# K loads of a later step issued behind both turnings of the key blocks, other slots within a step, and another order of the begin

## The chip, the cores and the metric

The kernel runs on one core of a Trainium2 chip. The metric is the device time of one execution in microseconds (us). TensorE (PE) multiplies matrices, VectorE (DVE), ScalarE (ACT) and GpSimd (POOL) work on tiles, and SyncE (SP) issues nearly all the DMAs of this kernel, one behind the other.

## The reference

Three layers in a chain, over B=4 batches, H=8 heads, S=768 positions and D=48 columns, which are 3072 tokens of 384 columns for the two layers behind.

```
k_n = k / (np.linalg.norm(k, axis=-1, keepdims=True) + 1e-06)
for t in range(S):
    y[:, :, t] = np.einsum('bhd,bhde->bhe', q[:, :, t], state)
    v_old = np.einsum('bhde,bhd->bhe', state, kt)
    state = state + bt[:, :, :, None] * np.einsum('bhd,bhe->bhde', kt, vt - v_old)
...
p = domain_probs / (domain_probs.sum(-1, keepdims=True) + 1e-09)
for e in range(E):
    h = np.maximum(x @ w1[e], 0.0)
    out += p[:, e:e + 1] * (h @ w2[e])
...
expert_idx = np.argmax(logits, axis=1)
for e in range(E):
    mask = expert_idx == e
    h = np.maximum(x[mask] @ w1[e], 0.0)
    out[mask] = gate_w[mask, None] * (h @ w2[e])
```

The first layer is attention by the delta rule. The second is a mixture of 4 experts, all of which see every token. The third has 8 experts, and each token goes to the one that its logits choose.

## The kernel before, in words

The attention is cut into 12 steps of 64 positions. Within a step the recurrence is solved for all positions at once: the Gram matrix of the keys (`gram_k`, L312) gives a triangular system, which DVE inverts in small pivots (`inverse`, L417 and L421), and products with the inverse give z, y and w (`solve_z`, `solve_y`, `solve_w`, L457). What leaves a step are its outputs (`outputs`, L576 and L579, then `columns`, which casts them into the tile xT, L163 and L164) and the new state (`state`, `keep_state`, L561 to L565). Numbers are kept as pairs of f16 halves, hi and lo, so that nearly every product is three matmuls.

The dense layer has 16 pieces per step (4 experts by 4 parts), and each piece is a first product (`first`, L900, with the ReLU on ACT, L904, and its low half on DVE, L905) and a second one (`second`, L922, with the sum into acc on DVE, L932). The dense pieces of one step are what PE does while the next step's attention is prepared. A step has 32 slots, two around each dense piece:

```
for i in range(16 * NS):
    ...
    if i % 16 < 15:
        hidden(i + 1)
    for g in at[2 * i]:
        g()
    dense.second(i, H.pop(i))
    for g in at[2 * i + 1]:
        g()
```

Every engine runs what it is given in the order of this loop; nothing is scheduled later. Which piece of the attention, of the routing or of the weights stands at which slot is written in tables at the head of the file: SLOTS for a step, SECOND for step 1, ROUTE for the routing of the sparse layer, WSLOTS for the third layer's weights, DENSE and KINDS for the splitting of the 32 weight tiles of the dense layer in the first interval (KINDS names the engines: in A, ACT makes the high half and a scaled copy and POOL the low half; in B, ACT makes the high half and DVE the low one; in C, ACT makes the high half, POOL the scaled copy and POOL the low half). WAYS names the engine that spreads results into block form ("S" a DMA of SP, "A" a copy on ACT, "V" a copy on DVE). ORDER is the order of the steps of the begin, before the first dense piece. A negative slot counts back from the start of its own step's interval.

The pieces that bear on the step boundary are these. `load_k` loads the keys of the following step into Kr (L176, 8 DMAs on SP). `split_k` cuts keys into halves KB (ACT L236, then DVE or POOL L238), for two halves x of the heads. `turn_k` turns KB[x] into KTB[x] by one transposing DMA of SP (L288). `sum_k` adds the halves of KTB on DVE into KQ (L305), and `gram_k` multiplies on PE (L312). `expand(0)` (e0) and `expand(1)` (e1) spread the solved columns Ws into WB (L525 on SP, L527 on ACT, L532 on DVE), which `outputs` reads. In the begin, `split_t` makes the halves TB of the inverse (ACT L446, DVE L450), and phi and plo make those of the masked products PT (ACT L385, POOL L388). Of the third layer's weights, wst is loaded (L1090), split on ACT (L1096, L1097) and POOL (L1098), and stored to DRAM as wimg (L1103).

Of the kernel before, what the change touches and what calls it, by code (L numbers as in the profile page):

```python
# [17 lines left out]

SLOTS = dict(load_k=-6, load_q=16, load_v=36, norm=(2, 2, 3, 4), split_k=(-24, -7), turn_k=(-14, -5),
             sum_k=(-5, -1), gram_k=(-2, 0), to_lanes=0, scale=0, split_g=(1, 4), split_q=(-4, -4), turn_q=0,
             gram_q=(5, 6), split_p=(8, 7), expand_s=(8, 10, 12, 14), init=5, pivots=(4, 6, 3, 3, 5, 5, 2, 3, 0),
             from_lanes=13, split_t=15, rest=(15, 17), z=19, save=19, y=21, e0=22, w=24, e1=24, state=25, keep=25,
             out=28)

SECOND = dict(load_k=0, load_q=18, load_v=34, norm=(14, 17, 17, 18), split_k=(-14, -7), turn_k=(-11,
              -7), sum_k=(-5, -1), gram_k=(-2, 0), to_lanes=0, scale=1, split_g=(7, 11), split_q=(-4, -4), turn_q=-3,
              gram_q=(9, 10), split_p=(12, 13), expand_s=(4, 3, 7, 8), init=1, pivots=(4, 0, 4, 0, 4, 1, 4, 4, 1, 2,
              5, 2), from_lanes=13, split_t=15, rest=(10, 16), z=17, save=17, y=19, e0=25, w=21, e1=22, state=24,  # L30
              keep=26, out=30)

ROUTE = dict(first=(0, 4, 7, 9, 9, 10, 10), rest=(2, 6, 11, 16, 20, 24, 27))
WAYS = dict(e0="S", e1="A", sb="SSAA", apply="V", klow="PV")
WSLOTS = dict(back=0, six=(7, 10, 13, 18, 20, 27), seven=(4, 7, 11, 13, 18, 20, 27))


HEAD = dict(loads=(2, 4, 7, 14, 21))
KINDS = "AAADABABABBBABBAABAABACCABCABBBB"
DENSE = dict(w=(0, 0, 1, 1, 1, 2, 3, 3, 3, 5, 6, 7, 7, 9, 10, 11, 13, 15, 15, 15, 16, 17, 20, 21, 22, 23,  # L40
             25, 25, 26), r=13, t=23, e=22, c=26, i=21, p=5, load=0, keep=1)


ORDER = """
cq cw ck0 zk1 load0 twin zk0 ck1 v0 za load1 zt zs0 zk2 load2 zw units square root scale square1 heads wide0 wide1
khi0 klo0 khi1 klo1 tk00 tk01 sum00 sum01 tk10 tk11 sum10 sum11 gd0 gd1 lanes lscale go0 go1 qhi0 qhi1 qscale zs1
tree tf0 root1 W00 W01 P P P P P P P P P P n1 n2 side qrest0 qrest1 n3 n4 n5 heads1 P P P P P wide10 wide11 tf1
khi10 klo10 khi11 klo11 gq0 q1 gq1 ag0 ag1 tk100 load3 tk101 tk110 tk111 mask0 phi0 mask1 P P P P P P P P P P P P
plo0 phi1 plo1 P P P P lanesback thi0 thi1 thi2 thi3 tlo0 tlo1 tlo2 sidelo tlo3 q1hi0 q1hi1 q1lo0 q1lo1 tq1 gate z
W02 save sum100 y e00 ylo v1 load4 e01 e02 e03 W20 W21 W22 sum101 w e10 gk0 sum111 gk0o e11 e12 e13 out0 W10 W11 W12  # L50
out1 columns sum110
"""


class Attention:
# [166 lines left out]
    def norm_apply(self):  # L222
        K = self.K
        eng = self.nc.gpsimd if WAYS["apply"] == "P" else self.nc.vector
        eng.tensor_tensor(out=K, in0=K, in1=self.r0.unsqueeze(2).to_broadcast([128, 16, 48]), op=ALU.mult)
# [4 lines left out]
    def split_k(self, s, x):  # L230
        nc, KB = self.nc, self.keys(s)[x]
        for q in range(4):
# [3 lines left out]
            nc.scalar.activation(out=hi, in_=src, func=AF.Copy)  # L236
            low = self.nc.gpsimd if WAYS["klow"][x] == "P" else self.nc.vector
            low.tensor_tensor(out=KB[r, 1, :, 64 * h:64 * h + 48], in0=src, in1=hi, op=ALU.subtract)  # L238
# [279 lines left out]
    def expand(self, f):  # L518

        for q in range(4):  # L520
            dst, src = self.part_w(f, q)
            how = WAYS["e1" if f else "e0"]
            if how == "S":
# [68 lines left out]
    def pieces(self, s):  # L592
# [5 lines left out]
        def at(slot, *fs):  # L598
            for f in fs:
                p.append((slot, f))  # L600
# [11 lines left out]
        each = lambda f: [lambda x=x: f(x) for x in two]  # L612
        P = SLOTS if s > 1 else SECOND
        if s > 1:
            N = SECOND if s == 2 else SLOTS
            for x in two:
# [15 lines left out]
        for n in range(4):  # L632
            f = self.expand_s if s > 1 and WAYS["sb"][n] == "A" else self.expand_d
            at(P["expand_s"][n], lambda n=n, f=f: f(*divmod(n, 2)))
# [763 lines left out]
def kernel(ctx, tc, q, k, v, beta, probs, w1, w2, emb, tau, v1, v2, out, NA=6):  # L1398
# [16 lines left out]
    def loads(lo, hi):  # L1415
        for n in range(lo, hi):
            dense.load_w(n, nc.sync)

    def head_loads(i):
        loads((0, *HEAD["loads"])[i], HEAD["loads"][i])  # L1420
        if i == 4:
            dense.load_p()
# [12 lines left out]
    at[0].append(attn.state_first)  # L1435
    at[DENSE["keep"]].append(attn.keep_first)
    for s in range(1, NS):
# [3 lines left out]
    for s in range(NS - 1):  # L1441
        for o, g in zip(ROUTE["rest"] if s < NS - 2 else ROUTE["first"], sparse.route_pieces(s, dense)):
            at[32 * (s + 1) + o].append(g)
    at[DENSE["load"]].append(lambda: loads(HEAD["loads"][-1], 32))
    for n, o in enumerate(DENSE["w"]):
        at[o].insert(n + 1 if o == 0 else len(at[o]), lambda n=n + 32 - len(DENSE["w"]): dense.split_w(n, KINDS[n]))
    at[DENSE["r"]].append(lambda: sparse.setup_d(sp, dense.ap))
    at[DENSE["r"] + 1].append(lambda: sparse.setup_r(sp, dense.ap))
    at[DENSE["t"]].append(sparse.setup_t)
# [10 lines left out]
    def w_load(n):  # L1460
        raw[n] = sparse.w_load(sp, *chunks[n])

    def w_split(n):
        cut[n] = sparse.w_split(sp, *chunks[n], raw.pop(n))

    def w_store(n):
        sparse.w_store(*chunks[n], cut.pop(n))
        if n + 2 < len(chunks):
            w_load(n + 2)

    at[29].append(lambda: (w_load(0), w_load(1)))
    six, seven = WSLOTS["six"], WSLOTS["seven"]
    slots = [32 * s + o for s in range(1, NS - 1) for o in (six if 2 <= s < 7 else seven)]
    for n in range(len(chunks)):
        at[slots[n]].append(lambda n=n: w_split(n))
        at[slots[n] + WSLOTS["back"]].append(lambda n=n: w_store(n))

# [127 lines left out]
```

## Time and profile before

| | |
|---|---|
| three runs | 1204.96, 1207.42, 1208.01 us, median 1207.42 |
| profiled execution | 1208.4 us, of which the span of its trace is 1206.7 |
| PE busy | 1125.0 us, 93% of the span |
| weight loads (PEld) | 877.8 us, 73% |
| DVE busy | 807.1 us, 67% |
| ACT busy | 656.7 us, 54% |
| POOL busy | 422.2 us, 35% |
| DMA from and to HBM | 148 GB/s over the span |

The span is the time from the first to the last instruction of the trace; the profiled execution's own time holds 1.7 us around it. Busy times are shares of the whole span. In the page's 40 slices PE is busy in nine tenths or more of each slice but the first ones, and its granted clock is full but for three of the first four (8, 5 and 8 tenths), where the begin and the first dense pieces lie.

### The profile page before, as it was taken

How to read it: one execution, taken by the hardware profiler on the slowest of the kernel's cores; microseconds unless marked ns; L12 is line 12 of the kernel's file. 1: busy time of each engine (PE TensorE's matmuls, PEld its weight loads, DVE VectorE, ACT ScalarE, POOL GpSimd, SP SyncE). 2: the span in 40 equal slices, each digit the busy share in tenths (PEclk: the TensorE clock that was granted, in tenths of full speed). 3: DMA queues.
4: the chain of work that ended last, by engine and by line, in shares of the span. 5: the costliest groups of instructions: out<-in, count | busy, mean ns of one | idle time of the engine just before them, and what ended most of it. 6: DMA issues, size and time to landing. Idle time of an engine off the chain costs nothing. (4 is left out here: it accounts for less than half of the span.)

```text
span 1206.7 us, 33186 instructions
## 1 busy us (share of the span) xinstructions
PE 1125.0 (93%) x12906; PEld 877.8 (73%) x12906; DVE 807.1 (67%) x2859; ACT 656.7 (54%) x1268; POOL 422.2 (35%) x394
## 2 busy tenths in 40 slices
PE   2488999999998999999999999999999999999997
PEld 2466677777777777777777777777777777788775
DVE  8778788687786877868779788797773543222121
ACT  6667675666666665666666675666553142222221
POOL 5647533251332523425135251342411213222221
PEclk8598999999999999999999999999999999999999
DMA  9983345644666346545565475565721195969951
GB/s 218 218 205 75 71 97 149 108 100 118 108 149 113 90 123 109 123 89 119 144 101 148 96 147 142 103 154 105 133 73 28 37 346 133 345 174 283 310 131 29
DMA packets 294672, 167.24 MB, mean 139 GB/s; under 512 B 241396, under 2 KB 276040, under 8 KB 294512
## 3 DMA queue, kind: packets, MB, share of 16 engines
q1 hardware_dynamic: 288656, 154.91, 55.6%
q0 software_dynamic: 4768, 9.98, 2.7%
q8 instruction: 103, 1.69, 0.6%
q14 instruction: 57, 0.47, 0.1%
q10 hardware_dynamic: 1088, 0.20, 0.1%
HBM read 142.54 MB, written 35.90 MB: 148 GB/s over the span
## 5 line engine op out<-in xcount | busy, mean ns | idle before, releaser
L900 PE MATMUL ph<-xT,W 128*128 128x256 f16 x2808 | 334.4, 274 | 4.0 <-POOL W L885 2.4
L922 PEld LDWEIGHTS <-H 128*128 128x128 f16 x2304 | 221.4, 98 | 138.1 <-issue 6.5
L922 PE MATMUL po<-W,H 128*128 128x384 f16 x1728 | 308.7, 328 | 5.1 <-DVE H L905 3.0
L900 PEld LDWEIGHTS <-W 128*128 128x128 f16 x2808 | 271.1, 98 | 45.5 <-POOL W L885 2.9
L904 ACT ACTIVATE H<-ph 128x512 f16<-128x512 f32 x192 | 113.2, 590 | 155.8 <-PE ph L900 151.0
L905 DVE SCALAR_TENSOR_TENSOR H<-ph,H 128x512 f16<-128x512 f32 x192 | 131.1, 686 | 78.0 <-ACT H L904 74.8
L1098 POOL TENSOR_TENSOR wso<-wst,wso 128x768 f16<-128x768 f32 x64 | 105.2, 1644 | 199.7 <-ACT wst L1097 192.3
L1373 DVE SCALAR_TENSOR_TENSOR H<-ph,H 128x512 f16<-128x512 f32 x54 | 37.4, 692 | 156.3 <-ACT H L1372 156.3
L1368 PE MATMUL ph<-xt,slot 128*128 128x128 f16 x1944 | 114.7, 221 | 4.0 <-DMA xt<-g 4.0
L1368 PEld LDWEIGHTS <-slot 128*128 128x128 f16 x1944 | 112.3, 99 | 7.9 <-issue 4.7
L421 DVE TENSOR_TENSOR tt<-tt,pr 128x60 f32<-128x60 f32 (+34 forms) x660 | 111.3, 209 | 0.7
L417 DVE TENSOR_TENSOR pr<-tt,KQ 128x60 f32<-128x60 f32 (+34 forms) x660 | 109.7, 203 | 0.8
L1385 PE MATMUL po<-slot,H 128*128 128x384 f16 x648 | 109.9, 326 | 0.0
L378 POOL TENSOR_TENSOR AO<-O,AO 32x256 f16<-32x256 f32 x48 | 47.0, 980 | 161.7 <-ACT AO L377 159.7
L922 PE MATMUL po<-Wlate,H 128*128 128x384 f16 x576 | 101.2, 326 | 0.7 <-DVE acc L932 0.7
L1096 ACT ACTIVATE wso<-wst 128x768 f16<-128x768 f32 x64 | 53.7, 840 | 71.0 <-DMA wimg<-wso 42.9
L1385 PEld LDWEIGHTS <-H 128*128 128x128 f16 x648 | 62.1, 98 | 38.3
L1390 POOL DMA_INDIRECT out_dram<-ob,idx x27 | 27.3, 1010 | 164.6 <-ACT ob L1389 125.7
L900 PE MATMUL ph<-xT,Wlate 128*128 128x256 f16 x648 | 78.2, 276 | 2.2 <-POOL Wlate L885 2.2
L1372 ACT ACTIVATE H<-ph 128x512 f16<-128x512 f32 x54 | 32.2, 597 | 80.9 <-PE ph L1368 80.9
L900 PEld LDWEIGHTS <-Wlate 128*128 128x128 f16 x648 | 63.3, 99 | 13.1 <-POOL Wlate L885 2.4
L1389 ACT ACTIVATE ob<-po,sm 128x384 f32<-128x384 f32 x27 | 15.7, 580 | 81.4 <-PE po L1385 81.3
(309 smaller groups left out, 1615.6 us busy)
## 6 DMA issues: line engine op xcount, KB each, us to landing
slot<-wimg SPq DMA_DIRECT2D x108, 768.0 KB
wst<-in_moe_w_dram SPq DMA_DIRECT2D x65, 384.0 KB
wimg<-wso SPq DMA_DIRECT2D x64, 384.0 KB
xb<-xr SPq DMA_DIRECT2D x48, 98.0 KB
Qr<-in_q_dram SPq DMA_DIRECT2D x24, 192.0 KB
Vr<-in_v_dram SPq DMA_DIRECT2D x96, 48.0 KB
W<-in_moe_w_dram SPq DMA_DIRECT2D x11, 384.0 KB
Kr<-in_k_dram SPq DMA_DIRECT2D x84, 48.0 KB
```

The costliest lines, as they stand in the source:

```text
L378: self.low.tensor_tensor(out=lo, in0=src, in1=hi, op=ALU.subtract)
L417: nc.vector.tensor_tensor(out=p, in0=t[:, :, j:j + 1].to_broadcast([128, m, j]), in1=AT[:, j, 0:j].unsqueeze(1).to_broadcast([128, m, j]), ...
L421: nc.vector.tensor_tensor(out=t, in0=t, in1=p, op=ALU.subtract)
L900: nc.tensor.matmul(ph[:, i], w1[:, a, k, 128 * i:128 * i + 128], xT[:, b, k], start=(n == 0), stop=(n == 8))
L904: nc.scalar.activation(out=H[:, 0], in_=ph, func=AF.Relu)
L905: nc.vector.scalar_tensor_tensor(out=H[:, 1], in0=ph, scalar=0.0, in1=H[:, 0], op0=ALU.max, op1=ALU.subtract)
L922: nc.tensor.matmul(po[t], H[:, a, i, 128 * t:128 * t + 128], w2[:, b, i], start=(f == 0 and i == 0 and n == 0), stop=(f == 3 and i == 1 an ...
L1096: self.nc.scalar.activation(out=o[:, 0], in_=t, func=AF.Copy, scale=scale)
L1098: self.nc.gpsimd.tensor_tensor(out=o[:, 1], in0=t, in1=o[:, 0], op=ALU.subtract)
L1368: nc.tensor.matmul(ph[:, i], w[:, a, k, 128 * (i % 2):128 * (i % 2) + 128], xt[:, 3 * b + k], start=(m == 0), stop=(m == 8))
L1373: nc.vector.scalar_tensor_tensor(out=H[:, 1], in0=ph, scalar=0.0, in1=H[:, 0], op0=ALU.max, op1=ALU.subtract)
L1385: nc.tensor.matmul(po, H[:, a, i], w[:, b, i % 2], start=(q == 0 and i == 0 and m == 0), stop=(q == 1 and i == 3 and m == 2))
```

## The change

Only the tables change; no instruction is written differently, and the sizes of all tiles stay. In a step, `load_k` goes from slot -6 to -3, behind the turning of the second half x (which stays at -5), the turning of the first half from -14 to -12, `split_k` from (-24, -7) to (-23, -6), `sum_k` of the first half from -5 to -7, the outputs from slot 28 to 29, and e0 from 22 to 24; other pieces move by a slot or a few. The spreading e0 goes from SP's DMAs to DVE copies, e1 from ACT copies to SP's DMAs. The weight tiles 11, 22 and 26 of the dense layer change kind, and many of them their slot (tile 26 from slot 21 to 20). In the begin, several steps trade places. The first lines of the tables, and those of the short ones:

```diff
-SLOTS = dict(load_k=-6, load_q=16, load_v=36, norm=(2, 2, 3, 4), split_k=(-24, -7), turn_k=(-14, -5),
+SLOTS = dict(load_k=-3, load_q=17, load_v=34, norm=(2, 2, 3, 4), split_k=(-23, -6), turn_k=(-12, -5),
...
-WAYS = dict(e0="S", e1="A", sb="SSAA", apply="V", klow="PV")
-WSLOTS = dict(back=0, six=(7, 10, 13, 18, 20, 27), seven=(4, 7, 11, 13, 18, 20, 27))
+WAYS = dict(e0="V", e1="S", sb="ASSA", apply="V", klow="PV")
+WSLOTS = dict(back=1, six=(7, 10, 12, 19, 22, 25), seven=(0, 6, 10, 13, 15, 24, 27))
...
-HEAD = dict(loads=(2, 4, 7, 14, 21))
-KINDS = "AAADABABABBBABBAABAABACCABCABBBB"
+HEAD = dict(loads=(2, 5, 5, 14, 19))
+KINDS = "AAADABABABBAABBAABAABAACABAABBBB"
```

SP at a step boundary before, from the spreading of w to the loads of V (Kr the keys of the next step but one, KB and KTB the halves and the turned keys of the coming step, xb rows of the dense layer's output that go out, wst and wimg the third layer's weights):

```order
L525 DMA WB<-Ws 32x8x48 x8
L176 DMA Kr<-in_k_dram 32x8x48 x8
L288 DMA_TRANSPOSE KTB_165<-KB_150 128x16x128
L1185 DMA xb<-xr_5220 64x392 x2
L1185 DMA xb<-xr_5221 64x392 x2
L1103 DMA wimg<-wso 128x1536
L1090 DMA wst<-in_moe_w_dram 128x3x256
L274 DMA_TRANSPOSE KQ<-QT 128x8x64 x4
L185 DMA Vr<-in_v_dram 32x8x48 x8
```

And the same place in the changed kernel:

```order
L525 DMA WB<-Ws 32x8x48 x8
L1103 DMA wimg<-wso 128x1536
L1090 DMA wst<-in_moe_w_dram 128x3x256
L288 DMA_TRANSPOSE KTB_165<-KB_150 128x16x128
L1185 DMA xb<-xr_5275 64x392 x2
L1185 DMA xb<-xr_5276 64x392 x2
L176 DMA Kr<-in_k_dram 32x8x48 x8
L274 DMA_TRANSPOSE KQ<-QT 128x8x64 x4
L185 DMA Vr<-in_v_dram 32x8x48 x8
```

The eight loads of K have moved from ahead of the transposition of KB to behind it and behind the four DMAs of xb. The eight DMAs of WB at the top are e0 before and e1 after.

ACT over the same stretch before, from the split of w (Ws) to the dense piece behind the split of K:

```order
L512 ACTIVATE Ws<-psw 64x384 x2
L527 ACTIVATE WB<-Ws 32x2x8x48 x4
L564 ACTIVATE SC_171<-S_169 128x384
L564 ACTIVATE SC_172<-S_170 128x384
L236 ACTIVATE KB_152<-Kr 32x8x48 x4
L904 ACTIVATE H<-ph 128x512
```

And in the changed kernel:

```order
L512 ACTIVATE Ws<-psw 64x384 x2
L904 ACTIVATE H<-ph 128x512
L1096 ACTIVATE wso<-wst 128x768
L1097 ACTIVATE wst<-wst 128x768
L564 ACTIVATE SC_171<-S_169 128x384
L564 ACTIVATE SC_172<-S_170 128x384
L904 ACTIVATE H<-ph 128x512
L236 ACTIVATE KB_152<-Kr 32x8x48 x4
```

The four copies into WB have left ACT, and a pair of weight splits and two ReLUs now stand ahead of the split of K.

ACT in the begin before, from the masked products to the first cast of z:

```order
L385 ACTIVATE PT_167<-Wlate 128x512
L385 ACTIVATE PT_168<-Wlate 128x512
L446 ACTIVATE TB<-H 32x16x16x2 x4
L259 ACTIVATE QT<-Qr 128x8x48 x2
L163 ACTIVATE Ws<-psz 128x384
```

And in the changed kernel:

```order
L385 ACTIVATE PT_167<-Wlate 128x512
L446 ACTIVATE TB<-H 32x16x16x2 x4
L259 ACTIVATE QT<-Qr 128x8x48 x2
L385 ACTIVATE PT_168<-Wlate 128x512
L163 ACTIVATE Ws<-psz 128x384
```

The second high half of PT has moved behind the four copies of TB and the two of QT; on POOL its low half (L388) follows it.

## Rows read from the trace of the kernel before

**Rows 1.** TensorE's waits by releaser: total us, times, longest.

```profile
PE ps L312 <- DVE KQ L305: 11.9, 8, 3.0
```

**Rows 2.** Timeline of TensorE: start, us, instruction, count, [idle before, releaser].

```profile
52.95 1.38 PE L312 MATMUL ps<-KQ,KTB 128*128 128x64 f16 x23 [0.42 <-DVE KQ L305]
...
236.49 1.72 PE L312 MATMUL ps<-KQ,KTB 128*128 128x64 f16 x24 [2.21 <-DVE KQ L305]
238.02 3.19 PE L922 MATMUL po<-W,H 128*128 128x384 f16 x12
...
389.65 1.39 PE L312 MATMUL ps<-KQ,KTB 128*128 128x64 f16 x24 [3.02 <-DVE KQ L305]
390.85 3.57 PE L922 MATMUL po<-W,H 128*128 128x384 f16 x12
...
466.93 1.17 PE L312 MATMUL ps<-KQ,KTB 128*128 128x64 f16 x24 [1.59 <-DVE KQ L305]
467.93 2.12 PE L922 MATMUL po<-W,H 128*128 128x384 f16 x12
```

**Rows 3.** A window's busy times: PE, PEld, DVE, ACT, POOL; clock, DMA.

```profile
390.40:393.80 3.40, 3.40 (x25) 1.88 (x22) 2.56 (x4) 2.19 (x7) 0.71 (x2) 0.50 1.16 185
```

**Rows 4.** Timeline of SP's queue at the boundary near 385 us.

```profile
364.28 5.70 SPq L525 DMA_DIRECT2D WB<-Ws  x8
375.20 3.79 SPq L176 DMA_DIRECT2D Kr<-in_k_dram  x8
379.09 4.24 SPq L288 DMA_TRANSPOSE KTB<-KB  x1
```

**Rows 5.** Timeline of VectorE at the same boundary.

```profile
372.26 2.90 DVE L238 TENSOR_TENSOR KB<-Kr,KB 32x384 f16<-32x384 f32 x4 [2.26 <-ACT KB L236]
...
382.57 1.14 DVE L932 SCALAR_TENSOR_TENSOR acc<-po,p,acc 128x384 f32<-128x384 f32 x2
389.17 0.76 DVE L305 TENSOR_TENSOR KQ<-KTB 128x512 f16<-128x512 f16 x2 [5.46 <-DMA KTB<-KB]
```

**Rows 6.** Timelines of SP and TensorE at the boundary before step 2.

```profile
144.84 1.71 SPq L288 DMA_TRANSPOSE KTB<-KB  x1
146.60 5.95 SPq L176 DMA_DIRECT2D Kr<-in_k_dram  x8
...
154.96 4.09 PE L900 MATMUL ph<-xT,W 128*128 128x256 f16 x36
158.88 0.86 PE L312 MATMUL ps<-KQ,KTB 128*128 128x64 f16 x24
```

**Rows 7.** Timeline of ScalarE ahead of the boundary at 464 us.

```profile
446.18 3.40 ACT L527 ACTIVATE WB<-Ws 32x768 f16<-32x768 f16 x4 [0.61 <-DVE Ws L515]
```

**Rows 8.** Timelines of POOL, ScalarE, VectorE and TensorE in the begin.

```profile
40.69 2.27 POOL L388 TENSOR_TENSOR PT<-Wlate,PT 128x512 f16<-128x512 f32 x2
40.77 0.63 ACT L385 ACTIVATE PT<-Wlate 128x512 f16<-128x512 f32 x1 [0.60 <-POOL Wlate L339]
41.31 2.60 ACT L446 ACTIVATE TB<-H 32x512 f16<-32x512 f32 x4
41.97 2.96 DVE L450 TENSOR_TENSOR TB<-H,TB 32x512 f16<-32x512 f32 x3 [1.43 <-ACT TB L446]
45.55 0.69 DVE L450 TENSOR_TENSOR TB<-H,TB 32x512 f16<-32x512 f32 x1
46.30 1.06 PE L457 MATMUL psz<-R,TB 128*128 128x48 f16 x22 [0.52 <-DVE TB L450]
```

**Rows 9.** Timelines of POOL and TensorE in the first interval.

```profile
114.32 0.20 PE L457 MATMUL psz<-R,TB 128*128 128x48 f16 x1 [4.94 <-ACT R L478]
116.02 4.01 PE L900 MATMUL ph<-xT,W 128*128 128x256 f16 x18
...
129.90 2.13 POOL L883 TENSOR_SCALAR Wlate<-Wlate 128x768 f32<-128x768 f32 x1 [2.04 <-issue]
134.17 3.40 PE L900 MATMUL ph<-xT,Wlate 128*128 128x256 f16 x16 [2.17 <-POOL Wlate L885]
```

More of the change, by code (lines that the diff above doesn't have):

```diff
@@ L17 @@
 DRAM = bass.MemoryType.DRAM
-SLOTS = dict(load_k=-6, load_q=16, load_v=36, norm=(2, 2, 3, 4), split_k=(-24, -7), turn_k=(-14, -5),
[L22 to L31, printed above, removed]
@@ L33 @@
-ROUTE = dict(first=(0, 4, 7, 9, 9, 10, 10), rest=(2, 6, 11, 16, 20, 24, 27))
-WAYS = dict(e0="S", e1="A", sb="SSAA", apply="V", klow="PV")
-WSLOTS = dict(back=0, six=(7, 10, 13, 18, 20, 27), seven=(4, 7, 11, 13, 18, 20, 27))
-HEAD = dict(loads=(2, 4, 7, 14, 21))
-KINDS = "AAADABABABBBABBAABAABACCABCABBBB"
-DENSE = dict(w=(0, 0, 1, 1, 1, 2, 3, 3, 3, 5, 6, 7, 7, 9, 10, 11, 13, 15, 15, 15, 16, 17, 20, 21, 22, 23,
-             25, 25, 26), r=13, t=23, e=22, c=26, i=21, p=5, load=0, keep=1)
-ORDER = """
@@ L45 @@
[L45 to L49, printed above, removed]
@@ L50 @@
-W02 save sum100 y e00 ylo v1 load4 e01 e02 e03 W20 W21 W22 sum101 w e10 gk0 sum111 gk0o e11 e12 e13 out0 W10 W11 W12
-out1 columns sum110
+SLOTS = dict(load_k=-3, load_q=17, load_v=34, norm=(2, 2, 3, 4), split_k=(-23, -6), turn_k=(-12, -5),
+             sum_k=(-7, -1), gram_k=(-2, 0), to_lanes=0, scale=3, split_g=(0, 3), split_q=(-6, -2), turn_q=-2,
+             gram_q=(5, 6), split_p=(9, 7), expand_s=(9, 10, 13, 15), init=5, pivots=(3, 6, 4, 4, 4, 4, 1, 5),
+             from_lanes=13, split_t=15, rest=(15, 18), z=20, save=21, y=21, e0=24, w=23, e1=24, state=25, keep=25,
+             out=29)
@@ new lines @@
+SECOND = dict(load_k=0, load_q=21, load_v=31, norm=(14, 17, 17, 18), split_k=(-14, -7), turn_k=(-11,
+              -3), sum_k=(-5, -1), gram_k=(-2, 0), to_lanes=1, scale=1, split_g=(7, 11), split_q=(-4, -4), turn_q=-3,
+              gram_q=(9, 10), split_p=(12, 13), expand_s=(6, 5, 9, 10), init=1, pivots=(3, 0, 4, 1, 6, 0, 5, 4, 0, 3,
+              5), from_lanes=12, split_t=15, rest=(9, 16), z=17, save=17, y=19, e0=26, w=21, e1=22, state=24, keep=26,
+              out=30)
+ROUTE = dict(first=(3, 3, 6, 9, 9, 11, 11), rest=(4, 6, 12, 16, 20, 23, 28))
@@ new lines @@
+WAYS = dict(e0="V", e1="S", sb="ASSA", apply="V", klow="PV")
+WSLOTS = dict(back=1, six=(7, 10, 12, 19, 22, 25), seven=(0, 6, 10, 13, 15, 24, 27))
+HEAD = dict(loads=(2, 5, 5, 14, 19))
+KINDS = "AAADABABABBAABBAABAABAACABAABBBB"
+DENSE = dict(w=(0, 0, 1, 1, 3, 3, 4, 4, 5, 5, 6, 7, 7, 9, 10, 11, 13, 15, 15, 16, 16, 17, 20, 20, 22, 24,
+             25, 25, 25), r=13, t=28, e=22, c=24, i=21, p=5, load=0, keep=1)
+ORDER = """
+ck0 load0 cw zk1 twin zk0 ck1 v0 cq load1 zt units square za root scale square1 heads wide0 wide1 khi0 klo0 khi1
@@ new lines @@
+klo1 tk00 tk01 sum00 sum01 zs0 load2 tk10 tk11 sum10 sum11 gd0 zk2 gd1 lanes lscale P zw go1 qhi0 qhi1 qscale zs1
+tree tf0 root1 W00 P W01 P P P P P P P n1 n2 side qrest0 P go0 qrest1 n3 n4 n5 heads1 P P P wide10 P wide11 tf1
+khi10 q1 P klo10 khi11 klo11 gq0 gq1 ag0 ag1 tk100 load3 tk101 tk110 P P P P P tk111 P P mask0 phi0 mask1 P P P P P
+P P plo0 P P lanesback thi0 thi1 thi3 thi2 tlo0 tlo1 sidelo tlo3 tlo2 q1hi0 q1hi1 q1lo0 q1lo1 tq1 phi1 plo1 gate z
+save W02 sum100 y e00 ylo W20 W21 v1 load4 e02 e01 e03 sum101 w e10 gk0 gk0o e11 e12 e13 out0 W10 W11 out1 W22
@@ L52 @@
+columns sum111 sum110 W12
 """
```

## The prediction, made before the result was known

> **What bounds the kernel now.** I read the busy shares first: TensorE is busy 93% of the span, so what can be won is what it waits. Then I read its waits by releaser. Beside those of the begin, the largest entry that returns is the Gram matrix of the keys, L312, waiting for the sum of the turned halves on VectorE, L305: eight waits, 11.9 us [rows 1]. One, of 0.42, is in the begin; the other seven, 11.5 us together, stand at step boundaries, and the timeline of TensorE shows three of them, 2.21, 3.02 and 1.59 [rows 2].
>
> A wait here costs more than its length. Undisturbed, the 24 matmuls of a Gram matrix take 0.86 [rows 6]; behind a wait they take 1.17, since the second half's sum comes while the first is multiplied, and after the waits of 2.21 and 3.02 they take 1.72 and 1.39, and the dense piece behind takes 3.19 and 3.57 where the third shows 2.12 [rows 2]. In the window behind the wait of 3.02 the granted clock is 0.50 [rows 3], which is 1.2 instead of 2.4 GHz. So the price of the seven is 11.5 + 5 x 0.31 (five waits without a clock loss) + 1.93 + 1.98 (two with one: 0.86 + 1.07, and 0.53 + 1.45) = **17.0 us**.
>
> Why VectorE is late, one boundary tells. It has nothing to do between the end of acc, 382.57 + 1.14 = 383.71, and the sum at 389.17, for which the DMA into KTB releases it [rows 5]. That transposition stands on SP behind the eight loads of K, which start at 375.20, when VectorE's split of KB has just ended (372.26 + 2.90 = 375.16), and take 3.79 to issue; the transposition is issued from 379.09 [rows 4, 5]. From there to the sum are 10.1 us, though its issue takes 4.24.
>
> **What the change does at a boundary.** The eight loads go behind the transposition: it can be issued when KB is ready. KB itself changes its time: its split stands one slot later, and a slot is (466.93 - 389.65) / 32 = 2.4 us [rows 2]; ScalarE loses the four copies into WB, 3.40 [rows 7], and gets about 2.3 ahead of the split (two passes over a weight tile and a ReLU). So KB is ready between 1.1 earlier and 2.4 later; I take 0.8 later, since the split's input waits for no slot but its engine's queue. The issue then comes 379.09 - 375.20 - 0.8 = 3.1 earlier. The second part is the data: the loads' packets no longer lie ahead of the transposition's. The issue of the loads bounds it by 0 to 3.8; I take 2, half. Together the sum comes 5 us earlier, more than the longest wait, 3.02. Nothing waits for the loads of K at their new place: they are split 12 slots, 29 us, on (from slot -3 to slot -23 of the step after).
>
> The Trainium skill, page "DMA: Bandwidth & Descriptors", section "Queues, rings and completion order", says that on each DMA engine descriptors are consumed in ring order. By it all of the loads' data stands ahead of the transposition's, and the order of issue is the order of the data; by the issue times alone only 3.1 would be won. The trace's 10.1 us from issue to sum, against an issue of 4.24, agrees with the ring order but does not prove it.
>
> What is late next is VectorE's own chain. The outputs go from slot 28 to 29, behind a dense piece that was in front of them, so 2.12 us of PE's work between outputs and Gram matrix are gone. The chain's end was at 383.71, and PE was free for the Gram matrix at 389.65 - 3.02 = 386.63: 2.9 of slack, less 2.1 is 0.8, less about 0.4 for the first half's sum is 0.4. The boundary before step 2 is a control for both: there the outputs already stand directly in front, the transposition is issued at 144.84 with the loads of K behind it at 146.60, and neither the 36 matmuls of the dense piece at 154.96 nor the Gram matrix at 158.88 wait [rows 6]. But there the low half of Q's split lay ahead of the outputs, and now it lies in the chain. I reserve **+2.0** for all boundaries (0 if the slack holds, +4.5 if each of eleven is 0.4 late).
>
> The engines of the spreadings, costed: e1 leaves ScalarE and becomes eight DMAs, 5.70 to issue [rows 4]; the outputs stand five slots, 12 us, behind, so 5.7 and some 2 to land leave about 4 us. e0 takes four copies on VectorE, which is busy 67%, five slots ahead of the outputs as well. I cost both at nothing; without that cover each costs its own length, once a step. The other slots (sums, pivots, weights, routing) I cost at nothing too: between boundaries TensorE has work queued, and its waits there are short.
>
> **The begin.** z starts its main part at 46.30, released by TB on VectorE [rows 8]. ScalarE's TB copies begin at 41.31, right behind the second high half of PT (40.77, 0.63), which had waited 0.60 for POOL. In the new order that pass comes later: 0.63 earlier at least. VectorE's three subtractions into TB take 2.96, though a single one takes 0.69: 0.9 too much, while POOL is in L388 from 40.69 to 42.96. With the second L388 moved behind, that falls away. Together **-1.5**; bounds -0.4 (the ScalarE part half hidden, VectorE as before) and -2.0.
>
> The Trainium skill, page "SBUF — State Buffer", section "SBUF: two separate sides", calls the port pair of VectorE and GpSimd an exclusive lock: the loser blocks for the whole instruction. The 2.96 that end right behind 42.96 plus two single lengths agree with it. By it the 0.9 is won in full, without it perhaps nothing, and the begin gives 0.6. It speaks against e0 as copies on VectorE too, where GpSimd works beside them.
>
> **The first interval.** TensorE waits 2.17 at 134.17 for the low half of a weight tile, and its 16 matmuls then take 3.40 [rows 9]; 36 undisturbed ones take 4.09 [rows 6], so 16 take 1.8 and 1.6 is lost to the clock. The tile is number 26, of kind C, with 2.13 on POOL for the scaled copy. It becomes kind A and stands a slot earlier: either would do. That is -3.8; a reserve of 1.0 for tiles 27 and 28, which move, gives **-2.7** (0 to -3.8). The wait of 4.94 at 114.32, behind which 18 matmuls take 4.01 [rows 9], ends with ScalarE's cast of R; its chain loses one low half on VectorE (tile 11) and one pass on ScalarE (tile 22), about 1 us each. I take **-1.1** (0 to -3).
>
> **Sum.** -17.0 + 2.0 - 1.5 - 2.7 - 1.1 = -20.3. From the profiled execution's 1208.4 (span 1206.7 and 1.7 around it) that gives 1188.1. The median of the runs shown, 1207.42, is 1.0 below the profiled one, so **1187**.
>
> **Rivals.** *Half of it.* Only the order of issue is won, and the split of KB is the full slot late: 3.9 - 2.4 = 1.5 earlier. Of the waits 3.02, 2.21 and 1.59, 1.5, 0.7 and 0.1 remain, for seven about 3, with the half sums' 0.31 seven times and one clock loss of 2: 7 us stay. 1194; if begin and first interval give nothing either, 1199. For it speaks the slot; against, the copies that leave ScalarE.
>
> *The chain on VectorE takes the wait over.* If outputs, Q's low half, acc and sum end 1.5 us too late at each of eleven boundaries, 16.5 us come back, and with the clock the time is 1204 to 1209: no change. It decides from 1.9 us of lengthening (0.4 slack). Against it stands the control [rows 6].
>
> *Slower: the outputs wait for e1's DMAs.* If the eight issues stand on SP behind a transposition and weight loads and land 7 us later than I take, TensorE waits 3 at each of ten steps, with a clock loss of 2 each (as for 3.02): 50 us less 20, but half of the steps would do: 1212. It decides when the landing is some 5.5 us late (1.5 waited and 1 to 2 of clock, ten times, is 25 to 35). Against it: SP is free from 369.98 to 375.20 behind e0's own DMAs, which leave [rows 4].
>
> **How the numbers follow.** This kernel's measurement can tell about 0.3%, 3.6 us, from no change. Forecast as summed 0.60, with its own range 1182 to 1193; half of it 0.24; the chain 0.08; slower 0.08. The range holds forecast and half-case: 1181 to 1201. Faster (below 1203.8) 0.85, within 0.3% 0.07, slower 0.08.
>
> **What would show it.** In the profile after: L312 waiting for L305 at no boundary but by tenths; the transposition issued within 1 us of the split's end and landing within 6; the loads of K behind xb; no window at half clock at a boundary; z's main part near 44.8; no wait for POOL near 134. I am wrong if the waits stay under another name: L900 waiting for xT, L576 or L579 for WB, or psz for R.

## The result, and the profile after

The changed kernel takes 1176.51 us (median of four runs, 1174.98 to 1178.80), the kernel before 1206.19 beside it: ratio 0.9755, 95% interval 0.9729 to 0.9780. It is faster by 29.7 us where 20.3 were forecast, and below the range. The profiled executions say the same: spans of 1177.0 and 1206.7. TensorE is busy for 1114.6 us instead of 1125.0, so 10.4 of the gain is busy time and 19.3 is idle time.

Read from the two timelines (the starts of the dense pieces, L900), the gain lies here, in us:

| stretch | change | forecast |
|---|---|---|
| begin, to the first dense piece (60.74, now 59.79) | -0.95 | -1.5 |
| first interval, to its end (154.96, now 149.72) | -4.29 | -3.8 |
| ten boundaries, each from the first dense piece of an interval to the fifth | -14.81 | -15.0 |
| the last four pieces of these ten intervals (nine of them gain) | -3.59 | 0 |
| the pieces between | -3.87 | 0 |
| last interval and last stage | -2.17 | 0 |

These are two single executions. Traces of kernels with the same tables differ by up to 0.8 in the begin and by 2 to 3 in the pieces between and in the last stage; the last four pieces repeat to 0.1 in the traces with the changed tables that have none of the pauses told of below.

The waits of TensorE by releaser in the changed kernel, with what answers to [rows 1] and the other large ones (columns as there):

```profile
PE psz L457 <- ACT R L478: 3.8, 1, 3.8
...
PE ps L312 <- DMA KQ<-QT: 2.3, 2, 1.4
...
PE ps L312 <- DVE KQ L305: 0.9, 2, 0.5
```

The 11.9 of [rows 1] are 0.9, of which one wait of 0.52 stands at a boundary. In exchange two waits of L312 for Q's transposition, 1.43 and 0.92, are new. The boundary of [rows 4, 5], now at 366 to 379 us, in the timelines of SP and then of TensorE:

```profile
365.95 2.92 SPq L288 DMA_TRANSPOSE KTB<-KB  x1
368.97 5.18 SPq L1185 DMA_DIRECT2D xb<-xr  x4
374.21 4.84 SPq L176 DMA_DIRECT2D Kr<-in_k_dram  x8
379.16 5.53 SPq L274 DMA_TRANSPOSE KQ<-QT  x4
```

```profile
372.31 4.09 PE L900 MATMUL ph<-xT,W 128*128 128x256 f16 x36
376.24 0.86 PE L312 MATMUL ps<-KQ,KTB 128*128 128x64 f16 x24
376.94 2.12 PE L922 MATMUL po<-W,H 128*128 128x384 f16 x12
```

The transposition is issued ahead of the loads, the Gram matrix follows the 36 matmuls without a wait and takes 0.86 instead of 1.39, and the piece behind takes 2.12 instead of 3.57 [rows 2]: at this boundary, in these two executions, 5.15 us.

The begin and the first interval, from the timelines that answer to [rows 8, 9]:

```profile
40.62 1.15 POOL L388 TENSOR_TENSOR PT<-Wlate,PT 128x512 f16<-128x512 f32 x1
40.49 2.62 ACT L446 ACTIVATE TB<-H 32x512 f16<-32x512 f32 x4 [0.39 <-DVE H L432]
41.17 1.86 DVE L450 TENSOR_TENSOR TB<-H,TB 32x512 f16<-32x512 f32 x2 [0.71 <-ACT TB L446]
43.65 1.41 DVE L450 TENSOR_TENSOR TB<-H,TB 32x512 f16<-32x512 f32 x2
45.12 1.06 PE L457 MATMUL psz<-R,TB 128*128 128x48 f16 x22 [1.24 <-DVE TB L450]
```

```profile
129.04 2.13 PE L900 MATMUL ph<-xT,Wlate 128*128 128x256 f16 x18
```

z starts its main part at 45.12 instead of 46.30, 1.2 earlier; the first two subtractions, one of them beside POOL's first pass, still take 1.86, against 1.41 for the two that run alone. The tile that TensorE had waited 2.17 for is there, and the 18 matmuls run at full clock.

### The profile page after: what moved, and what is told of

It is laid out like the page before. It is cut to its first block, busy times and chain, and to the rows that moved or that the text cites. A ratio compares the mean times of both kernels' runs of the same rounds, so it can differ in the third digit from the quotient of the medians.

```text
span 1177.0 us, 33182 instructions
## 1 busy us (share of the span) xinstructions
PE 1114.6 (95%) x12906; PEld 873.3 (74%) x12906; DVE 805.4 (68%) x2902; ACT 619.6 (53%) x1227; POOL 409.1 (35%) x393
## 5 line engine op out<-in xcount | busy, mean ns | idle before, releaser
L900 PE MATMUL ph<-xT,W 128*128 128x256 f16 x2808 | 334.0, 274 | 3.9 <-POOL W L885 2.4
L922 PEld LDWEIGHTS <-H 128*128 128x128 f16 x2304 | 219.4, 98 | 134.6 <-DVE H L905 5.1
L922 PE MATMUL po<-W,H 128*128 128x384 f16 x1728 | 306.5, 327 | 3.9 <-DVE H L905 1.7
L900 PEld LDWEIGHTS <-W 128*128 128x128 f16 x2808 | 273.3, 98 | 49.0 <-POOL W L885 2.7
L922 PE MATMUL po<-Wlate,H 128*128 128x384 f16 x576 | 101.3, 326 | 0.3 <-DVE acc L932 0.3
L378 POOL TENSOR_TENSOR AO<-O,AO 32x256 f16<-32x256 f32 x48 | 35.8, 745 | 125.6 <-ACT AO L377 122.9
L900 PE MATMUL ph<-xT,Wlate 128*128 128x256 f16 x648 | 76.7, 272 | 0.5 <-DVE Wlate L886 0.5
L900 PEld LDWEIGHTS <-Wlate 128*128 128x128 f16 x648 | 61.8, 98 | 9.5 <-DVE Wlate L886 0.7
```

Of the source, the lines that this page charges most:

```text
L378: self.low.tensor_tensor(out=lo, in0=src, in1=hi, op=ALU.subtract)
L900: nc.tensor.matmul(ph[:, i], w1[:, a, k, 128 * i:128 * i + 128], xT[:, b, k], start=(n == 0), stop=(n == 8))
L922: nc.tensor.matmul(po[t], H[:, a, i, 128 * t:128 * t + 128], w2[:, b, i], start=(f == 0 and i == 0 and n == 0), stop=(f == 3 and i == 1 an ...
```

## The experiments

Each group of runs stands on one chip, beside runs of the kernel before on it; a ratio is to those. Chips differ: the medians of the kernel before are 1204 to 1214 us on them.

**One number of the change.**

```diff
-SLOTS = dict(load_k=-6, load_q=16, load_v=36, norm=(2, 2, 3, 4), split_k=(-24, -7), turn_k=(-14, -5),
+SLOTS = dict(load_k=-3, load_q=16, load_v=36, norm=(2, 2, 3, 4), split_k=(-24, -7), turn_k=(-14, -5),
```

> The kernel before with one number changed: load_k from slot -6 to -3. Theory L (the loads' place on SP is what made TensorE wait at the boundaries): the seven waits of L312 for L305, 11.5 us, vanish with their half-sums and clock losses, some 13 to 17 us, 1189 to 1193 us, ratio 0.986 to 0.989. Theory E (the boundary was won by everything else that makes KB or the chain on VectorE earlier): within 0.3% of before, since KB, the outputs and the copies on ScalarE stay. Beside either: the loads now end later, and the squares of K (L199) in slot 2 read them; if that is the new wait of the changed kernel, ScalarE waits for Kr at one or two boundaries by 2 to 4 us and some 1 to 3 us come back.

Measured: 1195.51, ratio 0.9852 (0.9828 to 0.9876). Theory L: no wait of L312 for L305 is left at a boundary, and the ten stretches at the boundaries shrink by 17.4 in all (5.15 at the one shown above, as in the changed kernel). VectorE's split of KB and SP at that boundary:

```profile
367.69 2.90 DVE L238 TENSOR_TENSOR KB<-Kr,KB 32x384 f16<-32x384 f32 x4 [2.26 <-ACT KB L236]
```

```profile
370.66 1.73 SPq L288 DMA_TRANSPOSE KTB<-KB  x1
379.88 4.42 SPq L176 DMA_DIRECT2D Kr<-in_k_dram  x8
```

The transposition is issued 0.06 behind the end of the split, at this boundary and at eight others; in the kernel before it was 3.9 to 5.6 behind it at eight boundaries. The squares of K wait for Kr three times here, 1.9 together, so little comes back. One number gives some 18 of the 29.7 us.

**The same number taken out of the changed kernel.**

```diff
-SLOTS = dict(load_k=-3, load_q=17, load_v=34, norm=(2, 2, 3, 4), split_k=(-23, -6), turn_k=(-12, -5),
+SLOTS = dict(load_k=-6, load_q=17, load_v=34, norm=(2, 2, 3, 4), split_k=(-23, -6), turn_k=(-12, -5),
```

> The changed kernel with load_k back at slot -6, all else as changed. Theory L: the waits of L312 for L305 come back, and 10 to 17 us with them, 1187 to 1193 us. Theory E: the split of KB and the chain on VectorE are early enough by themselves: 1176 to 1180. Under both the squares of K no longer wait for Kr, which gives back 1 to 2 us.

Measured: 1230.27, ratio 1.0153 (1.0120 to 1.0186): slower than before, and far outside both theories' numbers. Its TensorE at a boundary, and the window behind the wait (columns as [rows 3]):

```profile
391.78 1.72 PE L312 MATMUL ps<-KQ,KTB 128*128 128x64 f16 x24 [3.62 <-DVE KQ L305]
393.31 4.03 PE L922 MATMUL po<-W,H 128*128 128x384 f16 x12
```

```profile
391.50:400.00 8.50, 8.09 (x58) 5.41 (x58) 3.00 (x5) 2.50 (x8) 1.32 (x2) 0.62 0.63 108
```

L312 waits nine times for L305, 23.6 together; two of these are in the begin. Of the seven at boundaries, six, of 2.8 to 4.4 us, have a clock of 0.50 behind them for about 3 to 6 us (0.62 is the mean of the longer window above), and four boundaries lose 6.5 to 7.4 each against the changed kernel. Some 15 us of the distance to it are not the loads' but that chip's (the pauses shown with the changed kernel's second run). SP at the boundary shown:

```profile
376.19 3.81 SPq L176 DMA_DIRECT2D Kr<-in_k_dram  x8
380.10 0.39 SPq L1103 DMA_DIRECT2D wimg<-wso  x1
380.53 0.43 SPq L1090 DMA_DIRECT2D wst<-in_moe_w_dram  x1
381.07 6.86 SPq L288 DMA_TRANSPOSE KTB<-KB  x1
```

In the changed tables a store of wimg and a load of wst stand ahead of the transposition too. So it is issued 4.9 behind the split of KB instead of 3.9 as in the kernel before, and its issue takes 6.86 instead of 4.24 [rows 4]: the loads in front cost more than before. What makes that issue longer isn't shown. The other edits do not replace the move; they rest on it.

**w a slot earlier, alone.**

```diff
-             from_lanes=13, split_t=15, rest=(15, 17), z=19, save=19, y=21, e0=22, w=24, e1=24, state=25, keep=25,
+             from_lanes=13, split_t=15, rest=(15, 17), z=19, save=19, y=21, e0=22, w=23, e1=24, state=25, keep=25,
```

> The kernel before with w alone moved from slot 24 to 23, so that a dense piece more stands between the product w and the state that reads its halves Ws. Theory W (the 48 matmuls into pss take 1.67 us instead of 1.37 because they start on the halves of Ws just as VectorE finishes them): 0.30 us less in each of nine steps, 2.7 us or 0.22%, and pss at 1.37 in the trace. Rival: pss is slow for the spreading copies on ScalarE that read Ws at the same time; then pss stays at 1.67 and the time within 0.1%.

Measured: 1211.17, ratio 0.9995 (0.9970 to 1.0020). The 48 matmuls into pss did become fast (13.7 us for all 480, from 15.3), as theory W says; ScalarE's copies still run beside them, so the rival is out. Nothing was won all the same: psw now waits for Y, 8.2 instead of 1.0.

```profile
PE psw L457 <- DVE Y L481: 8.2, 11, 1.6
```

In the same execution L312 waits 5.1 for L305 instead of 11.9. Whether w gives that, or the execution, one trace can't tell: these waits differ between executions (see the next run).

**The begin and the dense weights alone**: the tables HEAD, KINDS, DENSE and ORDER of the changed kernel in the kernel before.

> The kernel before with the tables HEAD, KINDS, DENSE and ORDER of the changed one, that is the begin and the splitting of the dense weights alone. If these make what the changed kernel gains up to the end of the first interval: the first dense piece 0.9 earlier, the end of the first interval 5.2 earlier, 1201 us, ratio 0.9955; the boundaries stay as before. If a part of the 4.3 in the first interval came from the moves of the attention's pieces there (table SECOND), 1203 to 1205.

Measured: 1207.81, ratio 0.9957 (0.9930 to 0.9983). By its trace the first dense piece comes 1.50 earlier and the end of the first interval 2.56 earlier, not 5.2: the first interval itself gains 1.06, not 4.29. The wait of 2.17 for the weight tile is gone, but TensorE waits there for another tile, the halves eh that the routing needs, and the matmuls behind take 4.00 instead of 2.15:

```profile
132.06 0.23 PE L1049 MATMUL ps<-ident,eh 8*128 8x8 f16 x3 [1.02 <-ACT eh L937]
133.78 0.24 PE L1049 MATMUL ps<-ident,eh 8*128 8x8 f16 x3 [1.50 <-DVE eh L938]
134.31 4.00 PE L922 MATMUL po<-Wlate,H 128*128 128x384 f16 x12 [0.28 <-DVE acc L932]
```

What takes these waits away in the changed kernel shows below, where the engines of the spreadings are set back. L312 waited 14.0 for L305 in this execution, against 11.9, though nothing at the boundaries was changed, so that a single trace says little of the total.

**Both edits together.**

> The kernel before with load_k at slot -3 and the tables HEAD, KINDS, DENSE and ORDER of the changed one. If the two gains add (1.48% and 0.43% by their own runs): ratio 0.981, about 23 us less, and 6.5 us of the changed kernel's 29.6 are left for the other slots. If the begin's part is only the drift of a single trace: 0.985.

Measured: 1188.41, ratio 0.9837 (0.9801 to 0.9873). The sum of the two, 0.981, lies inside the interval, and so does the loads' part alone.

**The routing's and the weights' slots of before in the changed kernel.**

```diff
-ROUTE = dict(first=(3, 3, 6, 9, 9, 11, 11), rest=(4, 6, 12, 16, 20, 23, 28))
-WSLOTS = dict(back=1, six=(7, 10, 12, 19, 22, 25), seven=(0, 6, 10, 13, 15, 24, 27))
+ROUTE = dict(first=(0, 4, 7, 9, 9, 10, 10), rest=(2, 6, 11, 16, 20, 24, 27))
+WSLOTS = dict(back=0, six=(7, 10, 13, 18, 20, 27), seven=(4, 7, 11, 13, 18, 20, 27))
```

> The changed kernel with the tables ROUTE and WSLOTS of before. Theory S (the 6 to 7 us that the two costed edits leave unexplained come from the weight splits standing elsewhere on ScalarE, which held up the ReLUs, the low halves on VectorE and y): 4 to 8 us slower than the changed kernel, ratio to before 0.979 to 0.982, with waits of L922 for H and of psw for Y between the boundaries. Rival: these tables don't matter, 0.9755 as the changed kernel.

Measured: 1225.81, ratio 1.0169 (1.0135 to 1.0204). Theory S's place is right, its size is six to twelve times too small: some 50 us by the ratios, 44 by the traces. Its waits, and one step of it on ScalarE, VectorE, POOL and TensorE:

```profile
PE psw L457 <- DVE Y L481: 16.1, 12, 1.6
...
PE psw L457 <- ACT Y L478: 9.7, 10, 2.2
```

```profile
282.30 0.84 ACT L1096 ACTIVATE wso<-wst 128x768 f16<-128x768 f32 x1 [3.95 <-DMA wimg<-wso]
283.18 0.84 ACT L1097 ACTIVATE wst<-wst 128x768 f32<-128x768 f32 x1
283.93 0.51 ACT L478 ACTIVATE Y<-Vr 128x384 f16<-128x384 f32 x1
```

```profile
284.47 1.74 DVE L481 SCALAR_TENSOR_TENSOR Y<-Vr,Y 128x384 f16<-128x384 f32 x1 [1.97 <-ACT Y L478]
```

```profile
284.15 1.64 POOL L1098 TENSOR_TENSOR wso<-wst,wso 128x768 f16<-128x768 f32 x1 [4.89 <-ACT wst L1097]
```

```profile
286.25 0.74 PE L457 MATMUL psw<-Y,TB 128*128 128x48 f16 x23 [1.59 <-DVE Y L481]
```

The weight split of slot 20 holds Y up twice in the step shown: ScalarE waits 3.95 for an earlier store of wimg before it, and its two passes stand ahead of Y's high half; then its pass on POOL lies beside Y's low half on VectorE, which takes 1.74. In ten of the twelve steps the low half takes 1.74 beside such a pass; in the changed kernel, without one, 0.56.

**The weights' slots alone.**

> The changed kernel with the table WSLOTS of before alone (ROUTE stays changed). Theory S now (w at slot 23 needs y early, and the weight split at slot 20 on ScalarE holds y's high half up, which costs 2 to 6 us a step with ROUTE and WSLOTS of before): psw waits for Y in nearly every step, 30 to 50 us slower than the changed kernel, ratio to before 1.0 to 1.017. If ROUTE was the cause: 0.9755 to 0.98.

Measured: 1247.62, ratio 1.0272 (1.0233 to 1.0311), beside 1195.32 and 0.9848 for the changed kernel on the same chip: 52 us by the medians. psw waits 17.1 for Y's low half and 8.4 for its high half. ROUTE is not needed for it.

**w at slot 24 in the changed kernel.**

```diff
-             from_lanes=13, split_t=15, rest=(15, 18), z=20, save=21, y=21, e0=24, w=23, e1=24, state=25, keep=25,
+             from_lanes=13, split_t=15, rest=(15, 18), z=20, save=21, y=21, e0=24, w=24, e1=24, state=25, keep=25,
```

> The changed kernel with w back at slot 24. The 48 matmuls into pss should take 1.67 us again instead of 1.37: 2.7 us slower than the changed kernel, 0.978, and no wait of psw for Y. If the outputs then wait for e1, which now follows w in the same slot, up to 10 us more, 0.978 to 0.986.

Measured: 1207.66, ratio 0.9939 (0.9915 to 0.9963), beside 1195.32 and 0.9848: 12 us by the medians, over four times the 2.7 of the forecast. TensorE waits nine times up to 1.4 for Ws ahead of pss:

```profile
PE pss L457 <- DVE Ws L515: 12.5, 9, 1.4
```

In the kernel before, w at 23 won nothing (w_early); here it is worth 12 us, where the weights' slots let Y come early.

**The weights' slots, w and the loads' place in the kernel before.**

> The kernel before with load_k at -3, w at 23 and the table WSLOTS of the changed one. w alone gave nothing (0.9995), since psw then waited for Y 8.2 us. If the weight split at slot 20 was why: the waits for Y go, and the time is that of the loads alone (0.9852) less 3 us for pss and up to 4 us for ScalarE's splits between the boundaries: 0.979 to 0.983. If not: 0.985 or above, with psw waiting for Y.

Measured: 1212.77, ratio 1.0007 (0.9981 to 1.0034). A miss: the waits for Y go, as expected, but L312 waits for L305 again, 14.5 us in seven waits. At one boundary, POOL and SP:

```profile
297.59 1.66 POOL L1098 TENSOR_TENSOR wso<-wst,wso 128x768 f16<-128x768 f32 x1 [2.15 <-issue]
```

```profile
299.27 0.35 SPq L1103 DMA_DIRECT2D wimg<-wso  x1
299.72 0.39 SPq L1090 DMA_DIRECT2D wst<-in_moe_w_dram  x1
300.21 5.49 SPq L288 DMA_TRANSPOSE KTB<-KB  x1
```

VectorE's split of KB ends at 297.01, and the transposition is issued 3.2 later: it stands on SP behind the store of wimg, which waits for the weight split of slot 25. In this kernel K is split in that same slot and comes first on ScalarE; in the changed kernel K is split a slot later, behind the weights. At five boundaries the transposition is issued 3.2 to 4.7 behind the split. The copies of e1, which are on ScalarE here, are not the reason: old_ways, below, has them there too, with K's split a slot later, and its transposition is issued 0.06 behind the split.

**The engines of the spreadings of before in the changed kernel.**

```diff
-WAYS = dict(e0="V", e1="S", sb="ASSA", apply="V", klow="PV")
+WAYS = dict(e0="S", e1="A", sb="SSAA", apply="V", klow="PV")
```

> The changed kernel with the table WAYS of before: e0 on SP's DMAs, e1 as ScalarE's copies. I costed the exchange at nothing. If that holds: ratio 0.974 to 0.978. If ScalarE's 3.4 us ahead of the split of K at slot -6 matter, KB is ready 3.4 later, the transposition too, and L312 waits 0.5 to 2 us at the boundaries, with the clock 10 to 30 us: 0.984 to 1.0.

Measured: 1190.53, ratio 0.9875 (0.9835 to 0.9915); the trace is 12.7 us longer than the changed kernel's, of which 5.2 lie in the pieces between, 4.3 at the boundaries and 2.3 in the first interval. I had costed the exchange at nothing; undone in the changed kernel it costs about 1.2% (the changed kernel's ratio is from another chip). L312 waits 4.3 for Q's transposition instead of 2.3 and L922 3.6 for H instead of 1.7. In the first interval the waits for eh of the begin alone are back, 1.02 and 1.50. ScalarE there:

```profile
126.91 3.39 ACT L527 ACTIVATE WB<-Ws 32x768 f16<-32x768 f16 x4
131.96 0.51 ACT L937 ACTIVATE eh<-em 8x384 f16<-8x384 f32 x1
```

In the changed kernel the copies are not on ScalarE, its half of eh starts at 130.58, and of the two waits one of 0.77 is left. So it is the exchange that gives the first interval most of what the begin's tables alone didn't.

**The changed kernel again, on two more chips.**

> The changed kernel itself once more, on the chip of the next three: 0.9755 of before, as measured. Its trace against the first one of it says how far waits at the boundaries and in the last stage differ between executions: I expect the two waits of L312 for Q's transposition again, and the last stage within 2 us.

> The changed kernel as the reference on the chip of the next three. 0.9755 of before if its blocks of outputs and Gram matrix take 3.7 us as in its first trace, 0.985 if they take 4.7 to 5.5 with gaps put down to issue, as in its second.

Measured: 1195.32, ratio 0.9848 (0.9809 to 0.9886), and 1175.75, ratio 0.9769 (0.9736 to 0.9803). The last stage of its first and its third execution differs by 2.66 us with the same tables, so the -2.17 of the table can't be put down to the change. The two waits of L312 for Q's transposition, which I expected again, are in the third (0.72 and 1.27) and not in the second. In the second one TensorE pauses within the block of the outputs:

```profile
295.74 0.23 PE L576 MATMUL psv<-KQ,SB 128*128 128x64 f16 x2 [0.41 <-issue]
296.49 0.27 PE L576 MATMUL psv<-KQ,SB 128*128 128x64 f16 x3 [0.43 <-issue]
297.02 0.86 PE L312 MATMUL ps<-KQ,KTB 128*128 128x64 f16 x24
```

Summed over the boundaries, the pauses make the stretches before them 1.5 to 1.8 longer, at ten of them 16 us.

**The outputs back at slot 28.**

```diff
-             out=29)
+             out=28)
```

> The changed kernel with the outputs back at slot 28, so that a dense piece stands between the outputs' 96 short matmuls and the Gram matrix's 24. Theory I (the joined block of 120 runs out of issued instructions on some chips): no gaps there on any chip; on a chip where the changed kernel has them, 12 to 16 us faster than it; on one where it hasn't, within 3 us. Rival: the gaps come with the chip, whatever the order; then as many gaps as the changed kernel beside it and the same time. If the slot was made to give the outputs' inputs time, L576 or L579 waits for WB or SB: 5 to 20 us slower.

Measured: 1197.29, ratio 0.9943 (0.9921 to 0.9966), beside 0.9769: 21 us slower, on a chip where the changed kernel shows no pauses, so theory I was not put to its test here. L576 and L579 wait for nothing new. L312 waits 10.6 in six waits for Q's transposition, and L922 6.4 for H; on ScalarE the squares of K (L199) wait 19.6 for Kr, instead of 5.3 in the changed kernel beside it:

```profile
PE ps L312 <- DMA KQ<-QT: 10.6, 6, 2.5
```

**The loads a slot earlier, still behind the transposition**, twice, and with the outputs at 28.

```diff
-SLOTS = dict(load_k=-3, load_q=17, load_v=34, norm=(2, 2, 3, 4), split_k=(-23, -6), turn_k=(-12, -5),
+SLOTS = dict(load_k=-4, load_q=17, load_v=34, norm=(2, 2, 3, 4), split_k=(-23, -6), turn_k=(-12, -5),
```

> The changed kernel with load_k at slot -4 instead of -3, that is directly behind the transposition and ahead of the four DMAs of xb. In the changed kernel's trace the squares of K wait for Kr by 3.6 and 2.1 us at two boundaries, and L312 waits 1.4 and 0.9 for Q's transposition behind the loads. If the loads only stand too late there: those four waits go, 2 to 4 us less than the changed kernel, 1173 to 1175 us. If their data then delays the sums instead, L312 waits for L305 again: 1178 to 1190.

> The changed kernel with load_k at -4, beside the changed kernel on one chip. If its first ratio (0.9724 against 0.9755 on another chip) is real: 3 to 4 us faster than changed_third, with no wait of the squares of K for Kr and none of L312 for Q's transposition. If it was the chip: the same.

> Both: load_k at -4 and the outputs at 28. If theory I and the loads' place hold and add, the fastest of all: 0.972 on a chip without the gaps, and the same 0.972 on one with them, where the changed kernel has 0.985. If the outputs' earlier slot lets them wait for e1, no better than loads_4.

Measured: 1171.51, ratio 0.9724 (0.9693 to 0.9756); 1172.55, ratio 0.9741 (0.9707 to 0.9774), beside 0.9769 of the changed kernel on the same chip; and 1175.61, ratio 0.9775 (0.9741 to 0.9809) with the outputs at 28. With the loads at -4 both waits for Q's transposition and those of the squares for Kr are gone from the traces. The kernel with the loads at -4 is 3.2 us ahead of the changed kernel by the medians on one chip; the intervals of the ratios overlap, so that it is better is likely and not shown. The outputs' slot hardly matters there, 3 us: on one chip, 21 us with the loads at -3 and 3 with them at -4, so the 21 us of out_28 hang on where the loads stand.

## Why the prediction was wrong

**Right, in mechanism and size: the boundaries.** Forecast 17.0, less a reserve of 2.0; the one number alone gives 17.4 at the boundaries by its trace and 18 by its median, with an interval from 15 to 21. The step "the eight loads go behind the transposition" is shown by loads_behind, and from the other side by loads_ahead. How much of it is issue and how much data (3.1 and 2 in the forecast) can't be read there: in loads_behind the sum at this boundary follows VectorE's other work without waiting for KTB. That the net fits so well, 14.8 for 15.0, is partly luck: the reserve was for VectorE's chain, and that was late once, by 0.52, which cost 1.0; another 1.6 went at a boundary with a wait for Q's transposition.

**Wrong reason for it: "Nothing waits for the loads of K at their new place".** I looked at the split, 12 slots on, and missed the squares of K in slot 2 (L199). In the changed kernel, at one boundary, SP and ScalarE:

```profile
223.19 9.94 SPq L176 DMA_DIRECT2D Kr<-in_k_dram  x8
233.26 5.29 SPq L274 DMA_TRANSPOSE KQ<-QT  x4
```

```profile
235.71 0.84 ACT L199 ACTIVATE ksq<-Kr 128x768 f32<-128x768 f32 x1 [3.60 <-DMA Kr<-in_k_dram]
```

Q's transposition stood behind the eight loads, and both L199 and L312 waited. Of the 9.94, 6.2 are not issuing but SP's own waits, three of them, for the landing of the xb and wst DMAs ahead of the loads. SP's waits in the changed kernel have a row that the kernel before doesn't have:

```profile
SPq L176 <- DMA xb<-xr: 18.7, 10, 3.8
```

In these traces nearly every DMA of SP uses again the semaphore of the DMA eight places ahead of it on the queue, and each load waits until that one has landed. So eight loads behind xb's four DMAs, wimg and wst wait for all of these. In loads_4, where the loads stand ahead of xb, the row and the waits of L199 are gone.

**The failed step: what I put at nothing, "The other slots (sums, pivots, weights, routing)" and the exchange of e0 and e1.** The stretches where I forecast no change hold 7.5 of the 9.4 us that the trace is beyond the forecast, the last four pieces 3.6 and the pieces between 3.9; the other 2 are the last stage, which differs as much between executions. What I took for full speed was a string of waits of tenths, most below what the list of waits names. The matmuls into pss, of the kernel before and after in the groups by line (busy, mean ns, idle before them):

```profile
L457 PE MATMUL pss<-Ws,KB 128*128 128x48 f16 x480 | 15.3, 184 | 1.2
```

```profile
L457 PE MATMUL pss<-Ws,KB 128*128 128x48 f16 x480 | 13.7, 183 | 0.0
```

That is 2.8 us in ten steps: their operand Ws was finished while they ran. And Y's low half on VectorE, before and after:

```profile
L481 DVE SCALAR_TENSOR_TENSOR Y<-Vr,Y 128x384 f16<-128x384 f32 x12 | 19.1, 1592 | 15.6 <-ACT Y L478 15.6
```

```profile
L481 DVE SCALAR_TENSOR_TENSOR Y<-Vr,Y 128x384 f16<-128x384 f32 x12 | 7.1, 595 | 8.5 <-ACT Y L478 8.5
```

POOL's pass of the weight split of slot 20 began 0.3 ahead of it in ten of the twelve steps and made it 1.74 instead of 0.56; the kernel before hid that by having w at 24. The change moves the weights, so Y is early, so w can stand at 23, so Ws is ready for pss. In the kernel before, w alone gives nothing (w_early), and with the weights' slots and the loads it even loses what the loads alone win (wslots_loads); taken out of the changed kernel, the weights' slots cost 52 us and w 12. That is why pricing the edits one by one, from the trace of before, gave zero. How much of the -3.87 between is owed to which slot stays open; old_ways puts 5.2 us on the exchange in these same pieces, so a good part may be the exchange's.

The Trainium skill, page "SBUF — State Buffer", section "SBUF: two separate sides", says that of a VectorE instruction with two SBUF inputs and a GpSimd instruction that reads SBUF, the one that starts first holds the shared port pair for the whole instruction. The rows agree: Y's low half, 0.56 alone, takes 1.74 when POOL's pass of 1.64 began 0.3 ahead of it, and ends 0.4 behind that pass.

**The begin and the first interval** came out at -0.95 and -4.29 for -1.5 and -3.8. In the begin ScalarE's copies start 0.8 earlier, for 0.63. VectorE's 0.9 was not won in full, because one POOL pass still lies beside the first subtraction, which takes 1.15 instead of 1.54, and 0.69 alone. Over all traces of this document the first dense piece starts at 59.2 to 59.8 with the new order of the begin and at 60.0 to 60.8 with the old one, about 1.0 apart. In the first interval both waits changed as forecast (the tile's 2.17 is gone, that for R is 3.80 instead of 4.94), but the sum fits by luck: with these edits alone the waits for eh came in their place and the interval gained 1.06. The rest needed the exchange, which I had at nothing.

**The exchange e0 and e1** is 1.2% in the changed kernel. The rivals: no half-case and no chain on VectorE appeared; the slower rival's wait, L579 for WB, did not occur at a boundary of the changed kernel.

**Not foreseen: the chip.** In one of its three measurements, on a chip of its own, the same kernel gains 1.5% instead of 2.3 to 2.5%. What tells the traces apart is the pauses put down to issue; their cause stays open, since out_28 ran where there are none. On the two chips that have them, the four kernels with the outputs directly ahead of the Gram matrix (changed_again, loads_ahead, old_wslots, w_late) pause for 8.6 to 12.4 us in all, and the four with a dense piece between (loads_behind, begin_alone, w_early, wslots_loads) for 2.1 to 4.3. That speaks for theory I, but these kernels differ in other slots too.

## What to carry to other kernels

A DMA that something waits for soon should not stand on its queue behind loads for later, and the whole list of readers of a moved load has to be looked up, not the next split alone. What the queue itself waits for belongs to it too: here SP's own waits show why the loads were slow at their new place. Where a table of slots moves many pieces, look for rows that are long without a wait beside them (an instruction at 1.7 that elsewhere takes 0.6, a group of matmuls some tenths over its pace): they are the slack that a second edit turns into time, and edits like these can be worth something only together, so undo them one by one from the changed kernel, not only add them one by one to the old one.

## What the runs showed of the hardware that was not expected

Eight DMAs of 48 KB take 3.8 to 6.0 us on SP at the boundaries of the kernel before, and up to 9.94 in the changed one; the difference at the longest is SP waiting for the landing of the DMAs eight places ahead, 6.2 us there. One transposing DMA of 128x16x128 takes from 1.7 us of issue (loads_behind, at 370.66) to 8.8 (loads_ahead, at 624.1, behind eight loads, a store and a load); why is not shown. In the first trace of the changed kernel the outputs' 96 matmuls and the 24 of the Gram matrix run as one block of 3.7 us; in its trace on another chip it is 4.7 to 5.5, with two or three pauses of some 0.45 put down to issue. Kernels with a dense piece between the two groups, on chips where others have the pauses, show fewer: most of them near the last boundaries, or, in w_early, mostly one of 0.2 a boundary. A wait is not always followed by a lower clock: in the kernel before, the clock is 0.50 for some 3 us behind the waits of 2.21 and 3.02, and stays at 1.0 behind one of 2.27, at 620.66.
